# Moving TensorE's operands to the head of SBUF, on multiples of 64 bytes, in a local-attention and FFN kernel

## The chip, the cores and the metric

The kernel runs on one core of one Trainium2 chip. The metric is the device time of one execution in microseconds (us). The kernel before takes 646.3 us, the median of 3 runs (646.12 to 647.43).

## What is computed

One sequence of 2,048 rows with 640 features goes through a layer norm. The normed rows feed two branches: local attention with 32 heads of 20 features, where each row attends to 8 rows at distances 0, 2, ..., 14 back, and a feed-forward network with 1,536 hidden features. The second branch gates the first.

```python
xn = layernorm(x)                                   # 2048 x 640
q, k, v = split(xn @ wqkv)                          # 640 -> 3 x 640, 32 heads of 20
logits[s, w] = q[s] . k[s - 2*w] * 20**-0.5         # w = 0..7, masked where s - 2*w < 0
s = (softmax(logits) @ v) @ wo                      # 640 -> 640
g = silu(silu(xn @ w1) @ w2)                        # 640 -> 1536 -> 640
out = x + s * g
```

Everything is float32 outside the kernel.

## The kernel before

**Tiling.** The rows are taken in 4 groups of 512 (2 halves, 2 parities, since the attention steps by 2). Within a group a row sits on one of 128 partitions and in one of T = 4 column blocks.

**Products in three parts.** To keep float32 accuracy with TensorE's one-pass float32r products, each operand is split into a high half (rounded to float32r) and a low half (the rest), and each product is made of three matmuls: high by high, low by high, high by low. TH and TL hold the two halves of the transposed activations (5 chunks of 128 features, 512 rows each), SH and SL those of the hidden FFN values (two of each, for even and odd chunks f), and the 7 weight slots WR hold a weight chunk's high half in columns 0 to 639 and its low half in columns 640 to 1279. TensorE reads nothing else but the transposes' operands (`ident`, XIN and O).

**The stages of a group g** and their matmuls (stationary operand, moving operand):

- `qkv_phase` (lines 589 to 591, and 541 for the first quarter): TH or TL stationary in blocks of 128 rows, a weight slot moving with 480 columns; 960 matmuls in all.
- `wo_phase` of the group before (lines 623 and 625, through `tm_mm`): TH or TL stationary, a weight slot moving, cut in 384 and 256 columns because a product row of 640 does not fit one PSUM bank. `wo_last` does the same for the last group, and its last block (line 712) runs 15 matmuls of 256 columns after 15 of 384.
- `ffn_phase`: first layer (lines 740 to 742) with 128 columns of a weight slot stationary and TH or TL moving with 512 columns; 720 matmuls. Second layer (lines 623 and 625) with SH or SL stationary and a weight slot moving in 384 and 256 columns. The `wo` and second-layer products together are 816 matmuls of 384 columns and 816 of 256, nearly always in turn.
- Transposes (lines 411, 514, 522): 190 of 128 columns, in float32, with XIN, O or `ident` stationary and `ident` moving.

That is 3,502 matmuls, of which 3,312 are float32r. Each is issued with a weight load of its own (3,502 rows on the PEld engine of the profile).

**Other engines.** VectorE (DVE) does the attention itself (scores at lines 459 and 462, values at 491 and 496), the low halves (416, 530, 356, 748), and the last products with the gate. ScalarE (ACT) writes the high halves (415, 526, 354, 746) and the activations. Weights come from HBM once, are split into halves by ACT and DVE (the first ten by ACT and GpSimd, POOL), stored as halves in HBM (SyncE's queue, SP) and reloaded by POOL's queue (line 346) for later groups.

**The order.** A planner, the class `Weave`, gets every operation with its engine, an estimated duration, what it reads and writes, and a priority; it simulates the five engines and emits every engine's instructions in the resulting order. TensorE's own order is that in which the operations were added. A matmul of n columns is estimated at `n / 2400 + 0.0155` us (`mm`). The planner sees names of tiles, not addresses.

**Addresses.** All SBUF tiles come from one pool, `sb`, with one buffer per tile. Addresses are given out in the order in which the lines of `local_attention_silu_ffn` allocate the tiles; each size is rounded up to 32 bytes. So the order of the lines 188 to 213 is the layout. The first tile, `ident`, starts at byte 16512 of each partition, and `epst`, of 4 bytes, at 17024. In the built program the operands of the float32r matmuls start here:

| tiles | first byte before | modulo 64 | modulo 256 |
|---|---|---|---|
| TH0, TH1, TL0, TL1 | 93984 to 124704 | 32 | 32 |
| SH0, SL0 | 149280, 151328 | 32 | 32 |
| SH1, SL1 | 153632, 155680 | 32 | 32 |
| weight slots 0 to 6 | 188128 to 218848 | 32 | 224 |

The slices that a matmul reads start at a multiple of 512 bytes in TH, TL, SH and SL, and at 0, 1536, 2560 or 4096 bytes (or, as stationary operand, at a multiple of 512) in a slot, so they have the same remainders as the tiles. `ident` is on a multiple of 64; XIN, O and nearly all other tiles are at 32 modulo 64.

Of the kernel before, what the change touches and what calls it, by code (L numbers as in the profile page):

```python
# [8 lines left out]
F32 = mybir.dt.float32  # L9
F32R = mybir.dt.float32r  # L10
# [4 lines left out]
P = 128  # L15
S, D, F, H, DH = 2048, 640, 1536, 32, 20
W = 8
DC, FC = D // P, F // P
NQ = 4
HQ = H // NQ  # L20
CQ = HQ * DH
J = 8
T = 4
TOK = T * P
# [5 lines left out]
RING = 7  # L30
# [134 lines left out]
def local_attention_silu_ffn(ctx: ExitStack, tc: tile.TileContext, x, wqkv, wo, w1, w2, out):  # L165
    nc = tc.nc
    pool = lambda name, bufs, **kw: ctx.enter_context(tc.tile_pool(name=name, bufs=bufs, **kw))
    sb = pool("sb", 1)
# [16 lines left out]
    def tiles(name, n, shape, dtype=F32):  # L185
        return [sb.tile(shape, dtype, name=f"{name}{i}") for i in range(n)]

    ident = sb.tile([P, P], F32, name="ident")
    epst = sb.tile([P, 1], F32, name="epst")
    mask = sb.tile([P, T, W], F32, name="mask")  # L190
    KV = tiles("kv", NQ, [P, 2, HALO + T, CQ])
    Q = tiles("q", NQ, [P, T, CQ])
    O = sb.tile([P, T, D], F32, name="o")
    TH = tiles("th", 2, [P, DC, TOK], F32R)
    TL = tiles("tl", 2, [P, DC, TOK], F32R)
    PR = sb.tile([P, 2, W, CQ], F32, name="pr")
    L = tiles("l", 2, [P, T, W, HQ])
    E = tiles("e", 2, [P, T, W, HQ])
    SH = [sb.tile([P, TOK], F32R, name="sh0")]
    SL = [sb.tile([P, TOK], F32R, name="sl0")]  # L200
    M = tiles("m", 2, [P, T, HQ])
    SH.append(sb.tile([P, TOK], F32R, name="sh1"))
    SL.append(sb.tile([P, TOK], F32R, name="sl1"))
    Z = tiles("z", 2, [P, 2, T, HQ])
    XIN = sb.tile([P, T, D], F32, name="xin")
    ST = tiles("st", 2, [P, 2, 6])
    MV = sb.tile([P, T, 2], F32, name="mv")
    SD = sb.tile([P, 2, T], F32, name="sd")
    G = sb.tile([P, T, D], F32, name="gate")
    XR = tiles("xr", 2, [P, D])  # L210
    SF = tiles("sf", 2, [P, TOK])
    WR = tiles("w", RING, [P, 2 * D], F32R)
    RAW = tiles("raw", 2, [P, D])
    ACC = [psum.tile([P, TOK], F32, name=f"acc{i}") for i in range(6)]
    ROT = [psum.tile([P, TOK], F32, name=f"rot{i}") for i in range(2)]
# [23 lines left out]
    def dve(n, fn, reads, writes, prio, lock=False):  # L239
        add("DVE", dv(n), fn, reads, writes, prio, lock)  # L240

    def act(n, fn, reads, writes, prio, table=None):
        add("ACT", ac(n), fn, reads, writes, prio, table=table)

    def pe(dur, fn, reads, writes):
        add("PE", dur, fn, reads, writes)
        clock[0] += dur
# [52 lines left out]
    def width(u):  # L300
        return 3 * CQ if u[0] == "q" else D
# [31 lines left out]
    def w_load():  # L333
# [5 lines left out]
        n = width(u)  # L339
        r = WR[s]  # L340
        both = r.rearrange("p (s d) -> p s d", s=2)[:, :, :n]
# [26 lines left out]
    def w_next(*want):  # L368
# [4 lines left out]
        s, n = i % RING, width(want)  # L373
        return WR[s][:, :n], WR[s][:, D:D + n], ("wh", s), ("wl", s)

# [9 lines left out]
    def ln_stats(t, after=()):  # L385
        st = ST[t % 2]
        ks = ("st", t % 2)
        for k in range(2):
            dve(320, lambda k=k: nc.vector.bn_stats(out=st[:, k, :], in_=XIN[:, t, k * 320:(k + 1) * 320]),
                [("xin", t), *after], [ks + (k,)], 1)  # L390
        dve(60, lambda: nc.vector.bn_aggr(out=MV[:, t, :], in_=st), [ks + (0,), ks + (1,)], [("mv", t)], 1)

    def ln_rstd(a, b):
        n = range(a, b)
        act(b - a, lambda: nc.scalar.activation(SD[:, 0, a:b], MV[:, a:b, 1], AF.Sqrt, bias=epst, scale=1.0),
            [("mv", t) for t in n], [("sd", t) for t in n], 0, "sqrt")
        dve(10, lambda: nc.vector.reciprocal(out=SD[:, 1, a:b], in_=SD[:, 0, a:b]),
            [("sd", t) for t in n], [("rs", t) for t in n], 1)

    def ln_apply(t):  # L400
        dve(320, lambda: nc.vector.tensor_scalar(  # L401
            out=XIN[:, t, :], in0=XIN[:, t, :], scalar1=MV[:, t, 0:1], scalar2=SD[:, 1, t:t + 1],
            op0=OP.subtract, op1=OP.mult), [("rs", t), ("mv", t)], [("xin", t)], 1, lock=True)

    def split_t(src, skeys, c, i):
# [6 lines left out]
        pe(0.54, turn, skeys, [kp])  # L412
        hi, lo = TH[i][:, c, :], TL[i][:, c, :]
        kh, kl = t_keys(i, [c], kinds=["th"]), t_keys(i, [c], kinds=["tl"])
# [5 lines left out]
    def evac_qkv(g, q, t, ps, kp):  # L420
        kv, qq = KV[q], Q[q]
        act(2 * CQ, lambda: nc.scalar.activation(
# [4 lines left out]
    def halo(g, q):  # L427
        h, par = groups[g]
        kv = KV[q]
        own = kv[:, :, HALO:, :]  # L430
# [22 lines left out]
    def scores(g, q):  # L453
        i = q % 2
        l, e, m, kv, qq = L[i], E[i], M[i], KV[q], Q[q]
        hk = halo_keys(q)
# [19 lines left out]
    def values(g, q):  # L476
        i = q % 2
        e, z, kv = E[i], Z[i], KV[q]
        hk = halo_keys(q)
# [28 lines left out]
    def first_quarter(i):  # L508
# [8 lines left out]
        def turn(t):  # L517
# [6 lines left out]
            for a, b, tp, kp in parts:  # L524
                v = tp[:, :(b - a) * P].rearrange("p (c n) -> p c n", n=P)
                act((b - a) * P, lambda a=a, b=b, v=v: nc.scalar.activation(TH[i][:, a:b, tsl(t)], v, AF.Copy),
                    [kp], t_keys(i, range(a, b), [t], ["th"]), 0)
            for a, b, tp, kp in parts:
                v = tp[:, :(b - a) * P].rearrange("p (c n) -> p c n", n=P)
                dve((b - a) * P, lambda a=a, b=b, v=v: nc.vector.tensor_tensor(  # L530
                    out=TL[i][:, a:b, tsl(t)], in0=v, in1=TH[i][:, a:b, tsl(t)].bitcast(F32), op=OP.subtract),
                    [kp] + t_keys(i, range(a, b), [t], ["th"]), t_keys(i, range(a, b), [t], ["tl"]), 0)

        def products(t, part):
            o, kp = ps[t]
            for k in part:
                for c in range(DC):
                    x, kx = (TL, "tl") if k == 1 else (TH, "th")
                    wh, wl, kh, kl = ws[c]
# [35 lines left out]
    def qkv_phase(g, i, io):  # L575
        for q in range(NQ):
            if g == 0 and q == 0:
                ps = first_quarter(i)
            else:
                ps = [bank() for t in range(T)]  # L580
                for c in range(DC):
                    wh, wl, kh, kl = w_next("q", q, c)
                    for t in range(T):
                        o, kp = ps[t]

                        def unit(c=c, t=t, o=o, wh=wh, wl=wl):
                            o = o[:, :3 * CQ]
                            hi, lo = TH[i][:, c, tsl(t)], TL[i][:, c, tsl(t)]
                            nc.tensor.matmul(o, hi, wh, start=c == 0, stop=False)  # L589
# [6 lines left out]
            if g == 0:  # L596
                add("POOL", 2.0, lambda q=q: nc.gpsimd.memset(KV[q][0:2, :, 0:HALO, :], 0.0), ["first"] if q else [],
                    [("halo", q, 1, 0), ("halo", q, 2, 0), ("halo", q, 3, 0), ("halo", q, 4, 0)], 1 + q)
# [42 lines left out]
    def wo_phase(g, i):  # L641
        banks = tm_banks()
        a, b = banks
        for c in range(DC):
            wh, wl, kh, kl = w_next("wo", c)
            for t in range(T):
                def one(c=c, t=t, wh=wh, wl=wl):
                    tm_mm(banks, t, TH[i][:, c, tsl(t)], wh, c == 0, False)
                    tm_mm(banks, t, TH[i][:, c, tsl(t)], wl, False, False)
                    tm_mm(banks, t, TL[i][:, c, tsl(t)], wh, False, c == DC - 1)  # L650
                pe(3 * TM, one, t_keys(i, [c], [t]) + [kh, kl], [a[t][1], b[t // 2][1]])
# [14 lines left out]
    def wo_last(g, i):  # L666
# [22 lines left out]
        def whole(t, cols):  # L689
            for k in range(3):  # L690
                for c in range(DC):
                    st = (TH, TH, TL)[k][i][:, c, tsl(t)]
                    tm_mm(banks, t, st, ws[c][k == 1], k + c == 0, k == 2 and c == DC - 1, cols)
# [23 lines left out]
    def ffn_phase(g, i, ix, io):  # L717
        nxt = g + 1 if g + 1 < NG else None
        ps = prev = None
        for f in range(FC + 1):  # L720
# [11 lines left out]
            if f < FC:  # L732
# [11 lines left out]
                w_done()  # L744
                sf, sh, sl = SF[s], SH[s], SL[s]
                act(TOK, lambda sh=sh, h=h: nc.scalar.activation(sh, h, AF.Silu), [kp], [("sh", s)], 0, "silu")  # L746
# [35 lines left out]
    add("POOL", 0.7, consts, [], ["consts"], 0)  # L782
    act(1, lambda: nc.scalar.activation(SD[:, 1, 0:1], epst, AF.Sqrt), ["consts"], [("rs", 0)], 0, "sqrt")
    slot = 0
# [38 lines left out]
```

## Time and profile before

| | |
|---|---|
| median of 3 runs | 646.3 us |
| the profiled execution, by its own clock | 645.65 us |
| its span, first to last instruction | 643.9 us |
| PE busy | 637.7 us, 3,502 matmuls |
| PEld busy (weight loads) | 577.3 us, 3,502 loads |
| DVE busy | 537.3 us |
| ACT busy | 206.5 us |
| POOL busy | 125.3 us |
| granted TensorE clock, mean | 0.999 |

How to read it: a matmul's duration in the profile (say 337 ns for 384 columns) reaches from its start to the modelled end of its last result, and overlaps the next matmul's. What a matmul costs in a row of matmuls is the step from its start to the next one's start. The timeline gives starts to 0.01 us from the start of the span; the trace holds them to 1 ns, and where a mean step is given it is taken over these.

### The profile page before, as it was taken

The numbers are of one execution on the slowest core, as the hardware profiler recorded it, in microseconds if no ns is written. First come the engines' busy times: TensorE is split into PE (matmuls) and PEld (weight loads), VectorE is DVE, ScalarE is ACT, GpSimd is POOL, SyncE is SP. The second block draws the span as 40 slices with busy tenths as digits, with TensorE's granted clock in tenths as the row PEclk, the third lists the DMA queues.
The fourth block names the chain that finished last, engine by engine and source line by source line (L and its number), as shares of the span: only waits on it lengthen the run. The fifth ranks groups of instructions, "written<-read, shape, count | busy, mean of one in ns | idle before, by whom it ended". The sixth has DMA issues, their size and how long they took to land.

```text
span 643.9 us, 9033 instructions
## 1 busy us (share of the span) xinstructions
PE 637.7 (99%) x3502; PEld 577.3 (90%) x3502; DVE 537.3 (83%) x532; ACT 206.5 (32%) x401; POOL 125.3 (19%) x171
## 2 busy tenths in 40 slices
PE   8999999999999999999999999999999999999997
PEld 7888899999889989999888999999988899899897
DVE  6699999999999989998939999999106999899714
ACT  5436453443534032324332122223313222233130
POOL 6410000001101331112222124111122213311100
PEclk9999999999999999999999999999999999999999
DMA  9999999677999988556699989865679996886522
GB/s 270 333 308 325 317 402 399 263 226 222 314 318 322 288 285 267 172 186 207 183 262 279 291 218 302 271 189 159 173 207 263 275 307 198 295 267 199 164 82 81
DMA packets 74010, 162.44 MB, mean 252 GB/s; under 512 B 5632, under 2 KB 46816, under 8 KB 73968
## 3 DMA queue, kind: packets, MB, share of 16 engines
q0 software_dynamic: 26672, 82.58, 45.0%
q1 hardware_dynamic: 47296, 79.29, 39.8%
q8 instruction: 27, 0.44, 0.3%
q14 instruction: 15, 0.12, 0.1%
HBM read 109.55 MB, written 34.16 MB: 223 GB/s over the span
## 4 chain that ended last, share of the span: by engine, by line
PE 98%; DMA 1%; DVE 0%; ACT 0%; SPq 0%; issue 0%
PE acc L623 22%; PE acc L625 15%; PE acc L589 10%; PE acc L590 10%; PE acc L591 10%; PE rot L742 9%; PE rot L740 9%; PE rot L741 9%; PE rot L411 2%; PE acc L541 2%; DMA pr<-in_A_wqkv_dram 1%; PE rot L522 0%; PE rot L712 0%; PE acc L514 0%; DVE xin L401 0%; ACT w L354 0%
## 5 line engine op out<-in xcount | busy, mean ns | idle before, releaser
L623 PE MATMUL acc<-w,sh 128*128 128x384 f32 x384 | 115.0, 337 | 0.0
L589 PE MATMUL acc<-w,th 128*128 128x480 f32 x300 | 114.7, 382 | 0.0
L590 PE MATMUL acc<-w,tl 128*128 128x480 f32 x300 | 113.4, 378 | 0.0
L591 PE MATMUL acc<-w,th 128*128 128x480 f32 x300 | 113.4, 378 | 0.0
L625 PE MATMUL acc<-w,sh 128*128 128x256 f32 x384 | 107.6, 280 | 0.0
L459 DVE TENSOR_TENSOR pr<-q,kv 128x2560 f32<-128x2560 f32 x32 | 91.7, 2864 | 11.4 <-DMA kv<-kv 11.0
L740 PE MATMUL rot<-th,w 128*128 128x512 f32 x240 | 95.8, 399 | 0.0
L742 PE MATMUL rot<-th,w 128*128 128x512 f32 x240 | 94.8, 395 | 0.0
L741 PE MATMUL rot<-tl,w 128*128 128x512 f32 x240 | 94.3, 393 | 0.0
L491 DVE TENSOR_TENSOR pr<-e,kv 128x2560 f32<-128x2560 f32 x32 | 90.3, 2821 | 0.7
L462 DVE TENSOR_REDUCE l<-pr 128x128 f32<-128x2560 f32 x32 | 90.0, 2813 | 0.2
L346 POOL DMA_DIRECT2D w<-half_q x52 | 37.3, 717 | 234.2 <-DMA raw<-in_A_wqkv_dram 93.6
L746 ACT ACTIVATE sh<-rot 128x512 fp32r<-128x512 f32 x48 | 28.7, 598 | 162.2 <-PE rot L742 162.1
L496 DVE TENSOR_TENSOR pr<-pr 128x1280 f32<-128x1280 f32 x64 | 79.3, 1240 | 1.1
L346 POOL DMA_DIRECT2D w<-half_w x72 | 38.5, 535 | 181.7 <-PE acc L625 101.3
L625 PEld LDWEIGHTS acc<-w,sh 128*128 128x128 f32 x384 | 72.2, 188 | 1.8
L623 PEld LDWEIGHTS acc<-w,sh 128*128 128x128 f32 x384 | 72.0, 188 | 1.7
L591 PEld LDWEIGHTS acc<-w,th 128*128 128x128 f32 x300 | 56.3, 188 | 8.5
L590 PEld LDWEIGHTS acc<-w,tl 128*128 128x128 f32 x300 | 56.3, 188 | 8.0
L589 PEld LDWEIGHTS acc<-w,th 128*128 128x128 f32 x300 | 56.3, 188 | 8.0
L623 PE MATMUL acc<-w,sl 128*128 128x384 f32 x192 | 58.7, 336 | 0.0
L742 PEld LDWEIGHTS rot<-th,w 128*128 128x128 f32 x240 | 45.1, 188 | 10.3
(84 smaller groups left out, 980.6 us busy)
## 6 DMA issues: line engine op xcount, KB each, us to landing
w<-half_w POOLq DMA_DIRECT2D x72, 640.0 KB, 5.6
w<-half_q POOLq DMA_DIRECT2D x52, 480.0 KB, 4.9
half_w<-w SPq DMA_DIRECT2D x24, 640.0 KB
half_q<-w SPq DMA_DIRECT2D x20, 480.0 KB
w<-half_wo POOLq DMA_DIRECT2D x15, 640.0 KB, 5.0
kv<-kv SPq DMA_DIRECT2D x16, 560.0 KB
kv<-kv SPq DMA_DIRECT2D x16, 420.0 KB
gate<-in_B_w_dram SPq DMA_DIRECT2D x16, 320.0 KB
```

Source lines behind the costliest of these rows:

```text
L459: dve(2560, lambda t=t: nc.vector.tensor_tensor(out=PR, in0=win(qq[:, t:t + 2, :], W, 0), in1=win(kv[:, 0, t:t + 2, :], W, CQ), op=OP.mult ...
L462: dve(2560, lambda t=t: nc.vector.tensor_reduce(out=l[:, t:t + 2].rearrange("p t w h -> p (t w h)"), in_=PR.rearrange("p t w (h d) -> p (t ...
L491: dve(2560, lambda t=t, v=v: nc.vector.tensor_tensor(out=PR.rearrange("p t w (h d) -> p t (w h) d", d=DH), in0=e[:, t:t + 2].rearrange("p ...
L496: dve(2 * n * CQ, lambda n=n: nc.vector.tensor_tensor(out=PR[:, :, 0:n, :], in0=PR[:, :, 0:n, :], in1=PR[:, :, n:2 * n, :], op=OP.add), [] ...
L589: nc.tensor.matmul(o, hi, wh, start=c == 0, stop=False)
L590: nc.tensor.matmul(o, lo, wh, start=False, stop=False)
L591: nc.tensor.matmul(o, hi, wl, start=False, stop=c == DC - 1)
L623: nc.tensor.matmul(a[t][0][:, :CA], st, w[:, :CA], start=first, stop=last)
L625: nc.tensor.matmul(b[t // 2][0][:, h * CB:(h + 1) * CB], st, w[:, CA:], start=first and h == 0, stop=last, skip_group_check=True)
L740: nc.tensor.matmul(h, wh[:, cs], TH[i][:, c, :], start=c == 0, stop=False)
L741: nc.tensor.matmul(h, wh[:, cs], TL[i][:, c, :], start=False, stop=False)
L742: nc.tensor.matmul(h, wl[:, cs], TH[i][:, c, :], start=False, stop=c == DC - 1)
```

## The change

Only the order of the allocations changes. `mv` (32 bytes) and `st0` (64) are put behind `epst`, so that TH starts at 17152; TH, TL and the seven slots follow, then SH1, SL1, `st1`, SH0, SL0, and behind them all the other tiles.

```diff
     ident = sb.tile([P, P], F32, name="ident")
     epst = sb.tile([P, 1], F32, name="epst")
+    MV = sb.tile([P, T, 2], F32, name="mv")
+    ST = [sb.tile([P, 2, 6], F32, name="st0")]
+    TH = tiles("th", 2, [P, DC, TOK], F32R)
+    TL = tiles("tl", 2, [P, DC, TOK], F32R)
+    WR = tiles("w", RING, [P, 2 * D], F32R)
+    SH = [None, sb.tile([P, TOK], F32R, name="sh1")]
+    SL = [None, sb.tile([P, TOK], F32R, name="sl1")]
+    ST.append(sb.tile([P, 2, 6], F32, name="st1"))
+    SH[0] = sb.tile([P, TOK], F32R, name="sh0")
+    SL[0] = sb.tile([P, TOK], F32R, name="sl0")
+    SD = sb.tile([P, 2, T], F32, name="sd")
     mask = sb.tile([P, T, W], F32, name="mask")
+    M = tiles("m", 2, [P, T, HQ])
+    Z = tiles("z", 2, [P, 2, T, HQ])
     KV = tiles("kv", NQ, [P, 2, HALO + T, CQ])
     Q = tiles("q", NQ, [P, T, CQ])
     O = sb.tile([P, T, D], F32, name="o")
-    TH = tiles("th", 2, [P, DC, TOK], F32R)
-    TL = tiles("tl", 2, [P, DC, TOK], F32R)
     PR = sb.tile([P, 2, W, CQ], F32, name="pr")
     L = tiles("l", 2, [P, T, W, HQ])
     E = tiles("e", 2, [P, T, W, HQ])
-    SH = [sb.tile([P, TOK], F32R, name="sh0")]
-    SL = [sb.tile([P, TOK], F32R, name="sl0")]
-    M = tiles("m", 2, [P, T, HQ])
-    SH.append(sb.tile([P, TOK], F32R, name="sh1"))
-    SL.append(sb.tile([P, TOK], F32R, name="sl1"))
-    Z = tiles("z", 2, [P, 2, T, HQ])
     XIN = sb.tile([P, T, D], F32, name="xin")
-    ST = tiles("st", 2, [P, 2, 6])
-    MV = sb.tile([P, T, 2], F32, name="mv")
-    SD = sb.tile([P, 2, T], F32, name="sd")
     G = sb.tile([P, T, D], F32, name="gate")
     XR = tiles("xr", 2, [P, D])
     SF = tiles("sf", 2, [P, TOK])
-    WR = tiles("w", RING, [P, 2 * D], F32R)
     RAW = tiles("raw", 2, [P, D])
```

In the built program after the change TH, TL, the slots, SH1 and SL1 start at 0 modulo 256, and SH0 and SL0 at 64 modulo 256. All the large tiles of the other engines (KV, Q, O, PR, L, E, XIN, `gate`, XR, SF, RAW) start at 224 modulo 256, so again at 32 modulo 64. The instructions of all five engines, their order and their waits are the same ones as before; only addresses differ. PSUM and HBM are laid out as before.

## The prediction

> **What bounds the kernel now.** I read the page first: the busy times, the granted clock, and the chain of work that ended last.
>
> ```profile
> PE 637.7 (99%) x3502; PEld 577.3 (90%) x3502; DVE 537.3 (83%) x532; ACT 206.5 (32%) x401; POOL 125.3 (19%) x171
> PEclk9999999999999999999999999999999999999999
> PE 98%; DMA 1%; DVE 0%; ACT 0%; SPq 0%; issue 0%
> ```
>
> PE is busy without a gap, at the full clock, and is 98% of the chain. Second, the list of waits of PE alone:
>
> ```profile
> PE rot L514 <- POOL ident masks.py:199: 1.4, 1, 1.4
> PE rot L522 <- DVE xin L401: 1.1, 1, 1.1
> ```
>
> Those are all, both in the first 8 us. Afterwards PE waits for no engine and no DMA, so the time is the sum of the steps from one matmul's start to the next one's. Third, the timeline of PE, to see what a step is (columns: start, duration, engine, line, operands). Two stretches of the second FFN layer of group 0, both with SH0 (chunks f = 2 and f = 6), and one of the qkv products:
>
> ```profile
> 85.49 0.34 PE L623 MATMUL acc<-w,sh 128*128 128x384 f32 x1
> 85.67 0.28 PE L625 MATMUL acc<-w,sh 128*128 128x256 f32 x1
> ...
> 86.39 0.34 PE L623 MATMUL acc<-w,sh 128*128 128x384 f32 x1
> ```
>
> ```profile
> 113.59 0.33 PE L623 MATMUL acc<-w,sh 128*128 128x384 f32 x1
> 113.76 0.28 PE L625 MATMUL acc<-w,sh 128*128 128x256 f32 x1
> ...
> 114.45 0.33 PE L623 MATMUL acc<-w,sh 128*128 128x384 f32 x1
> ```
>
> ```profile
> 195.57 0.37 PE L590 MATMUL acc<-w,tl 128*128 128x480 f32 x1
> 195.78 0.38 PE L591 MATMUL acc<-w,th 128*128 128x480 f32 x1
> 195.99 0.38 PE L589 MATMUL acc<-w,th 128*128 128x480 f32 x1
> 196.21 0.38 PE L590 MATMUL acc<-w,tl 128*128 128x480 f32 x1
> 196.43 0.38 PE L591 MATMUL acc<-w,th 128*128 128x480 f32 x1
> 196.65 0.37 PE L589 MATMUL acc<-w,th 128*128 128x480 f32 x1
> ```
>
> Three pairs of 384 and 256 columns take 0.90 us in the first stretch (300 ns a pair) and 0.86 in the second (287), although nothing differs but the weight slot, and the slots are alike modulo 512. Five steps of 480 columns take 1.08 us: 216 each, in a cycle of 211, 215, 214, 222, 218. Fourth, the end, where 256-column matmuls run alone:
>
> ```profile
> 638.26 1.32 PE L712 MATMUL rot<-w,th 128*128 128x256 f32 x10
> 639.42 0.73 PE L712 MATMUL rot<-w,tl 128*128 128x256 f32 x5
> ```
>
> One lasts 276 ns, so the five make (730 - 276) / 4 = 113.5 ns a step (113.3 by the starts in ns). Over the whole trace the mean steps are 231.0 ns for 512 columns, 216.0 for 480 and 293.2 for a pair (of 801 pairs 448 are near 287, 307 near 300).
>
> **What a step is made of.** The shortest frequent steps are 211 ns for 480 columns and 171 for 384: 40 ns for 96 columns, 0.417 ns a column. At that rate the columns alone need 213.3 ns (512), 200.0 (480), 266.7 (a pair) and 106.7 (256). What stands above it is 17.7 ns for each of 720 matmuls, 16.0 for 960, 26.5 for 816 pairs: 12.7 + 15.4 + 21.6 = **49.7 us** that are not columns. This fixed part is all that the change can touch on PE.
>
> It has a grain. The repeating steps, 113.3, 286.7, 300.0, 233.3 (the slower of two rhythms of 512 columns) and 1080 for five, are all multiples of 3.33 ns, the time of 8 columns, which is 32 bytes: just what all these operands start off a 64-byte mark. And the tail's 113.3 is 106.7 + 6.6, or 16 columns, 64 bytes, to within the clock of the trace.
>
> **The change, part by part.**
>
> 1. *Instructions, waits, queues.* None is added, removed or moved; no wait changes its engine. Cost nothing, by comparison of the two instruction lists.
>
> 2. *The moving operand on a 64-byte mark* (slots for 480, 384 and 256 columns, TH and TL for 512). No row shows a float32r operand on such a mark, so the price is bounded. One end is nothing: a stream that starts 32 bytes off costs no more than an aligned one. The far end is the whole fixed part, 49.7 us. A value between: if PE takes its stream in 64-byte pieces, a run of 16m columns covers m pieces when aligned and m + 1 when off, and the extra piece costs 16 columns, 16 x 0.417 = 6.7 ns. The nearest row, the tail at 106.7 + 6.6, shows just that, and no product's steps repeat at less than 6 ns above their columns. I take it: 3,312 x 6.7 ns = **22.1 us**.
>
> 3. *The stationary operand on a 64-byte mark.* Here rows exist, in float32: at half clock, weight loads of `ident` (aligned) and of XIN (32 off) both last 230 ns and the transposes step by 213.3 both times; at full clock those of XIN and O step by 108.4. So I take nothing. Bounds: no loss is excluded, since moving and stationary streams now start alike (0 and 0 modulo 256, before 224 and 32); a gain could be at most what part 2 leaves of the 49.7 us.
>
> 4. *Tiles of DVE, ACT and POOL.* Their remainder modulo 64 stays 32. I take nothing. Were DVE 1% slower or faster (5.4 us), its idle 106.6 us (643.9 - 537.3) and the slack of part 6 would hide it.
>
> 5. *DMAs.* A slot's destination goes from 224 to 0 modulo 256, the attention tiles from 32 to 224. A reload lands 5.6 us after issue (median) and PE never waits for one: nothing. Only the opening is uncovered: the first 10 us include loads of `pr` that make up the chain's 1% DMA; were these 5% longer or shorter, it would be 0.3 us, an estimate.
>
> 6. *What is late next.* DVE's order is fixed, and in the stretch from 32 to 322 us it is busy 274.7 of 290. If PE gets 3.4% faster (22.1 of 645.65), that stretch shrinks to 280, and DVE still fits. From 338 to 450 it is busy 108.4 of 112, which shrinks to 108.2: full, but each SL is written 2 to 8 us before PE reads it, and DVE idles behind it (3.4 us busy between 450 and 483). At the end, the last O is written 6.7 us before its transposes at 614 us; DVE works on that chain from 483, PE's 131 us shrink by 4.5, leaving 2.2. I put 1 us of new waits in the sum; with the fixed part wholly gone it would be 3 or 4.
>
> **Sum**, against the profiled execution's own 645.65 us (span 643.9): 645.65 - 22.1 + 1.0 = 624.6. The median of the runs is 0.65 higher, so I forecast **625.2 us**. If only the 8 columns of the offset are paid instead of 16, it is 11 us less gain: 636.
>
> **The rivals.**
>
> *No change (646).* The grain of 32 bytes may be the chip's own piece, or only its clock; then 32 modulo 64 was aligned already. For it: the aligned and unaligned weight loads of part 3 are alike, and the two pair rhythms of 287 and 300 ns occur with the same addresses modulo 512, so much of the fixed part is rhythm, not address. The Trainium skill speaks for this case: "SBUF — State Buffer", in the section on Door 1, gives SBUF lines of 16 bytes, on which all operands of the kernel before already start; by that the sum would be 645.65 - 0. No run here shows such a line.
>
> *A bigger gain (605).* Both streams pay a piece: 2 x 6.7 x 3,312 = 44.4 us, less 3.5 us of DVE waits: 605.4. For it: the loads of float32r operands last 188 ns, those of float32 140, so that path is not the one of part 3. Against it: part 3. The Trainium skill, "TensorE: Matmul & The Clock Gate", section on the back-to-back issue gap, has warm bf16 matmuls step by N/2.4 + 2.5 ns, 215.8 for 512 columns where this trace has 231.0; by that rule all but 3,312 x 2.5 = 8.3 us of the 49.7 would go, 604.3 before waits.
>
> *Slower (653).* The fixed part depends on how a matmul's stream falls against the next one's weight load, which starts some 3 ns after it (PEld and PE starts). The trace shows two rhythms for the same work: 287 or 300 ns a pair, 229 or 233.3 for 512 columns. With all operands on one remainder the pairs may lock to the slow one: 801 x (300 - 293.2) = 5.4 us and 720 x (233.3 - 231.0) = 1.7 us, 645.65 + 7.1 + 0.65 = 653.4; were the 480-column steps all at the 222 of their cycle, 960 x 6 = 5.8 us more, 659. It decides as soon as the slow share of pairs, now 307 of 801, rises and the piece of part 2 is not real. Against it: the rhythm now follows the history and not an address (SH0's pairs are slow at f = 2 and fast at f = 6).
>
> **How the numbers follow.** The forecast's case, between 612 and 640, gets 0.38; the bigger gain 0.12; no change 0.14; slower 0.36, of which a quarter beyond 655. The range 605 to 655 leaves out about 0.07 below and 0.09 above. Faster by over 0.2% (about what a measurement of this kernel can tell from no change): 0.38 + 0.12 = 0.50.
>
> **What would show it.** The 480-column steps should fall from 216 to about 209 ns, those of 512 from 231 to 224, the pair from 293 to 280, the tail from 113.3 to 107 or to the 108.4 of the transposes, where weight loads may bind. If the steps move by 13 ns, both streams pay; if they stay and the time too, 64 is not the number; if the pairs all read 300, the rhythm decided. PE's list of waits should stay near 2.5 us; rows of DVE there would mean that part 6 was too mild.

## The result and the profile after

The changed kernel takes **644.0 us** (median of 6 runs, 643.8 to 644.53), the one before beside it 646.57 (6 runs, 646.12 to 647.43): a ratio of **0.9959, 95% interval 0.9946 to 0.9972**. The forecast had the direction and eight times the size: 21 us were expected, 2.6 came. A later comparison made it smaller still (last experiment).

The page of the changed kernel: busy times, granted clock, chain.

```profile
PE 635.4 (99%) x3502; PEld 576.0 (90%) x3502; DVE 536.6 (83%) x532; ACT 206.1 (32%) x401; POOL 126.5 (20%) x171
PEclk8999999999999999999999999999999999999999
PE 98%; DMA 1%; DVE 0%; ACT 0%; SPq 0%; issue 0%
```

The list of waits of PE, whole:

```profile
PE rot L523 <- DVE xin L402: 2.3, 1, 2.3
PE rot L515 <- POOL ident masks.py:199: 1.4, 1, 1.4
```

PE is still the only bound, it waits for nothing after the opening, and its busy time is 2.3 us less. So the difference is in the steps. The timeline of PE in the changed kernel (start, duration, engine, line, operands) at the places shown for the one before: second FFN layer with SH0 at f = 2 and f = 6, and qkv products (the seventh step's end is the last line).

```profile
85.59 0.34 PE L624 MATMUL acc<-w,sh 128*128 128x384 f32 x1
...
86.46 0.33 PE L624 MATMUL acc<-w,sh 128*128 128x384 f32 x1
...
113.69 0.34 PE L624 MATMUL acc<-w,sh 128*128 128x384 f32 x1
...
114.55 0.33 PE L624 MATMUL acc<-w,sh 128*128 128x384 f32 x1
```

```profile
150.20 0.38 PE L592 MATMUL acc<-w,th 128*128 128x480 f32 x1
...
151.72 0.37 PE L590 MATMUL acc<-w,th 128*128 128x480 f32 x1
```

Three pairs take 0.87 and 0.86 us, so both stretches run at 287 to 290 ns a pair. Over the whole trace the mean pair hardly moved: 293.2 ns before, 292.8 now. Seven steps of 480 columns take 1.52 us, 217 each: not the 209 that the forecast wanted but slightly more than before. The steps that fell are those of 512 columns, here in one steady stretch of each kernel (not at the same place of the order), the changed one first and an execution of the one before (run `b2` below) second:

```profile
112.26 0.39 PE L742 MATMUL rot<-tl,w 128*128 128x512 f32 x1
...
113.17 0.39 PE L743 MATMUL rot<-th,w 128*128 128x512 f32 x1
```

```profile
75.65 0.40 PE L741 MATMUL rot<-tl,w 128*128 128x512 f32 x1
...
76.58 0.40 PE L742 MATMUL rot<-th,w 128*128 128x512 f32 x1
```

Four steps: 0.91 us against 0.93, 227 against 233 ns. Over the whole traces the mean steps went from 231.0 to 228 ns (512 columns) and from 216.0 to 216.8 (480). The tail went the wrong way too:

```profile
638.27 0.76 PE L713 MATMUL rot<-w,tl 128*128 128x256 f32 x5
```

Five matmuls of 256 columns take 0.76 us where they took 0.73: 120 ns a step by the starts, before 113.3.

**What the steps follow.** Call the *distance* of a matmul the first byte of its moving operand less that of its stationary one, modulo 256. The change did not only bring the operands to multiples of 64, it also changed the distances:

| | before | after |
|---|---|---|
| 480 columns, `wo` pairs (slot over TH, TL) | 192 | 0 |
| 512 columns (TH, TL over slot) | 64 | 0 |
| pairs over SH1, SL1 | 192 | 0 |
| pairs over SH0, SL0 | 192 | 192 |

Three theories went into the experiments. **Mark**: the remainder modulo 64 of an operand sets the step (the forecast). **Distance**: the distance does. **History**: the same operations fall into different rhythms by how a stretch is entered, whatever the addresses.

The time of each part of PE's order, in us, from the starts in the traces (matmuls 0 to 109; the rest of qkv; FFN without its last ten matmuls; `wo` of groups 0 to 2; those ten and `wo_last` up to its last block; that block and the end), for the kernels of this document:

| kernel | opening | qkv | FFN | `wo` 0-2 | last `wo` | rest | span |
|---|---|---|---|---|---|---|---|
| before, first trace | 25.16 | 201.00 | 341.56 | 52.90 | 15.00 | 8.27 | 643.88 |
| before, `b1` | 25.21 | 201.00 | 341.46 | 54.46 | 15.00 | 8.29 | 645.42 |
| before, `b2` | 25.36 | 201.00 | 341.54 | 54.45 | 15.00 | 8.29 | 645.64 |
| before, `b3` | 24.94 | 201.00 | 341.40 | 54.48 | 15.00 | 8.29 | 645.11 |
| before + 32 bytes, `e2` | 24.72 | 201.02 | 341.10 | 52.15 | 15.00 | 8.27 | 642.26 |
| after | 25.67 | 201.66 | 339.15 | 53.34 | 14.66 | 8.29 | 642.76 |
| after, `a2` | 24.64 | 201.66 | 339.17 | 54.05 | 14.66 | 8.29 | 642.48 |
| after + 32 bytes, `e1` | 24.99 | 201.61 | 339.42 | 54.30 | 14.66 | 8.29 | 643.28 |
| `x1`, all SH at 192 | 25.20 | 201.66 | 338.42 | 53.32 | 14.70 | 8.30 | 641.60 |
| `x2`, all SH at 0 | 25.28 | 201.62 | 340.22 | 53.32 | 14.66 | 8.27 | 643.38 |
| `x3`, slots 128 from TH | 25.39 | 203.51 | 344.65 | 52.13 | 14.37 | 8.30 | 648.36 |
| `x4`, qkv weights at 12 | 25.01 | 199.35 | 338.46 | 53.30 | 14.70 | 8.30 | 639.11 |
| `x5`, qkv weights at 36 | 26.01 | 207.56 | 338.40 | 53.25 | 14.70 | 8.32 | 648.23 |

The opening varies by 1 us between executions of one kernel (25.67 and 24.64 of after), so it is left out of the readings. Nor is all of the `wo` column steps of PE. The second matmul of each of the three stages is held until ACT has emptied the PSUM bank that it writes, as the waits of the weight loads (PEld) show, here in the kernel before:

```profile
PEld acc L625 <- ACT q L425: 0.8, 3, 0.3
```

That is about 0.25 us for each stage. In `b3`, `a2` and `e1` the hold of the first stage is longer, and PE itself waits 0.7, 0.6 and 0.9 us there. The first `wo` stages of `a2` and `e1` take 18.50 and 18.75 us by this, where all the other stages of the two, and of the changed kernel's first trace, take 17.76 to 17.79.

### The profile page after: what moved, and what is told of

Its sections match the earlier page's. It is cut to its first block, busy times and chain, and to the rows that moved or that the text cites. A ratio compares the mean times of both kernels' runs of the same rounds, so it can differ in the third digit from the quotient of the medians.

```text
span 642.8 us, 9033 instructions
## 1 busy us (share of the span) xinstructions
PE 635.4 (99%) x3502; PEld 576.0 (90%) x3502; DVE 536.6 (83%) x532; ACT 206.1 (32%) x401; POOL 126.5 (20%) x171
## 4 chain that ended last, share of the span: by engine, by line
PE 98%; DMA 1%; DVE 0%; ACT 0%; SPq 0%; issue 0%
PE acc L624 22%; PE acc L626 15%; PE acc L590 10%; PE acc L592 10%; PE acc L591 10%; PE rot L742 9%; PE rot L743 9%; PE rot L741 9%; PE rot L412 2%; PE acc L542 2%; DMA pr<-in_A_wqkv_dram 1%; PE rot L523 0%; PE rot L713 0%; PE acc L515 0%; DVE xin L402 0%; ACT w L355 0%
## 5 line engine op out<-in xcount | busy, mean ns | idle before, releaser
L460 DVE TENSOR_TENSOR pr<-q,kv 128x2560 f32<-128x2560 f32 x32 | 90.2, 2820 | 11.4 <-DMA kv<-kv 10.9
L741 PE MATMUL rot<-th,w 128*128 128x512 f32 x240 | 94.9, 395 | 0.0
L743 PE MATMUL rot<-th,w 128*128 128x512 f32 x240 | 93.7, 391 | 0.0
L492 DVE TENSOR_TENSOR pr<-e,kv 128x2560 f32<-128x2560 f32 x32 | 90.3, 2821 | 0.7
L497 DVE TENSOR_TENSOR pr<-pr 128x1280 f32<-128x1280 f32 x64 | 76.5, 1195 | 1.1
L417 DVE TENSOR_TENSOR tl<-rot,th 128x512 fp32r<-128x512 f32 x35 | 23.9, 682 | 36.4 <-ACT th L416 36.3
```

The source lines that it names most:

```text
L460: dve(2560, lambda t=t: nc.vector.tensor_tensor(out=PR, in0=win(qq[:, t:t + 2, :], W, 0), in1=win(kv[:, 0, t:t + 2, :], W, CQ), op=OP.mult ...
L492: dve(2560, lambda t=t, v=v: nc.vector.tensor_tensor(out=PR.rearrange("p t w (h d) -> p t (w h) d", d=DH), in0=e[:, t:t + 2].rearrange("p ...
L497: dve(2 * n * CQ, lambda n=n: nc.vector.tensor_tensor(out=PR[:, :, 0:n, :], in0=PR[:, :, 0:n, :], in1=PR[:, :, n:2 * n, :], op=OP.add), [] ...
L741: nc.tensor.matmul(h, wh[:, cs], TH[i][:, c, :], start=c == 0, stop=False)
L743: nc.tensor.matmul(h, wl[:, cs], TH[i][:, c, :], start=False, stop=c == DC - 1)
```

## The experiments

**The mark alone, both ways (`e1`, `e2`).** Every float32r operand 32 bytes further on, off the mark in the changed kernel and onto it in the one before, all distances kept.

```diff
# e1, in the changed kernel
+    pad0 = sb.tile([P, 8], F32, name="pad0")
     TH = tiles("th", 2, [P, DC, TOK], F32R)
...
+    pad1 = sb.tile([P, 8], F32, name="pad1")
     SD = sb.tile([P, 2, T], F32, name="sd")
# e2, in the kernel before
+    pad0 = sb.tile([P, 8], F32, name="pad0")
     mask = sb.tile([P, T, W], F32, name="mask")
```

> The kernel after with 32 bytes put ahead of TH and 32 ahead of SD: all float32r operands start 32 bytes off a 64-byte mark again, but keep their distances from each other; the other large tiles stay at 32 modulo 64. Theory M (the 64-byte mark counts): the steps go back to those of before, 231 ns for 512 columns and 216.0 for 480, time about 646.5. Theory D (the distance between the moving and the stationary start, modulo 64, 128 or 256, counts): the steps stay as after, near 228 for 512 and 216.8 for 480, time about 644. Theory H (no address counts, only the history of the opening): any mixture.

> The kernel before with 32 bytes put ahead of mask: all tiles move by 32 bytes, so the float32r operands stand on 64-byte marks, with the distances of before (weight slots 192 bytes behind TH, modulo 256). Theory M: steps as after, 228 ns for 512 columns and 216.8 for 480, about 644. Theory D: steps as before, 231 and 216.0, about 646.5. Theory H: any mixture.

Measured: `e1` 644.58 us (5 runs), ratio to the kernel before 0.9957 (0.9943 to 0.9971), and `e2` 644.14 us (4 runs, 643.94 to 644.44), ratio 0.9958 (0.9943 to 0.9973). The steps stay with the distances: 480 columns 216.7 ns in `e1` (216.8 after), 216.02 in `e2` (216.0 before); 512 columns 229.0 (228.2 after) and 230.7 (231.0). So the mark moves no step, and the theory behind the forecast falls. What `e2` did gain is mostly in one column of the table: `wo` takes 52.15 us where `b2` takes 54.45. The timeline of PE in the `wo` stage of group 1, `e2` first, then `b2`, then the changed kernel:

```profile
362.79 0.33 PE L624 MATMUL acc<-w,th 128*128 128x384 f32 x1
...
363.65 0.33 PE L624 MATMUL acc<-w,th 128*128 128x384 f32 x1
```

```profile
365.25 0.34 PE L623 MATMUL acc<-w,th 128*128 128x384 f32 x1
...
366.15 0.34 PE L623 MATMUL acc<-w,th 128*128 128x384 f32 x1
```

```profile
363.62 0.34 PE L624 MATMUL acc<-w,tl 128*128 128x384 f32 x1
...
364.50 0.34 PE L624 MATMUL acc<-w,tl 128*128 128x384 f32 x1
```

Three pairs take 0.86, 0.90 and 0.88 us. `e2` and `b2` both have the distance 192 and still differ, 287 and 300 ns a pair; the changed kernel, at 0, has 293. Here history counts.

**TensorE alone (`m1`, `m2`, `m3`, `m4`).** Programs that leave out all of the reference's work (x is copied to the output) and in which only TensorE works, in rows of equal matmuls, with three transposes between rows: start offsets of both operands (`m1`), sizes and types (`m2`), the distance in steps of 4 bytes and beyond 256 and the entry of pairs (`m3`), all 64 distances (`m4`).

```diff
# m4, the rows of one distance m
+    for m in range(0, 256, 4):
+        row((512,), m, 0, 26)
+        row((480,), m, 0, 26)
+        row((384, 256), m, 0, 14, 512)
+        row((384, 256), m, 0, 14, 400)
```

> Nothing of the reference's work is done: x is copied to the output, and TensorE runs rows of 10 to 16 float32r matmuls of 512, 480, 384 and 256 in turn, and 384 columns, with the moving operand and the stationary operand each starting at 0, 32, ..., 224 bytes modulo 256 (64 combinations for each size), three transposes apart. Theory M: the step depends on each start modulo 64 alone; combinations with both on a mark are the shortest. Theory D: the step depends on the difference of the two starts and is the same along each diagonal. Theory H: the steps are alike in all 64 to about 1 ns, or differ without order. If the other engines are what makes the fixed part, all steps here come near n x 0.417 + 2 or 3 ns (215 for 512).

> Nothing of the reference's work is done: x is copied to the output, and TensorE runs rows of 24 float32r matmuls of 128 to 512 columns in steps of 32, of 512, 480, 384 and 256 columns with 32, 64 and 96 stationary columns, and of bf16 operands, each with both starts at 0 and at 32 bytes. If the fixed part of a step is a piece of the moving stream, it is the same 7 ns for any number of stationary columns and appears only at 32. If it comes from the weight load that runs beside the matmul, it shrinks with the stationary columns: from about 17 ns at 128 to about 13, 9 and 4 at 96, 64 and 32. If it belongs to float32r's four bytes, bf16 shows 2 to 3 ns.

> Nothing of the reference's work is done. TensorE runs rows of 22 float32r matmuls of 512 and of 480 columns with the stationary operand at 0 and the moving one at 0, 4, ..., 64 bytes and at 128 to 1024, and rows of 14 pairs of 384 and 256 columns at distances 192, 0 and 32, each row after 3 matmuls of another size (256 to 512 columns in steps of 16) that shift its entry. Theory D with a period of 256 bytes: distances 256, 512, 768 and 1024 read like 0, and 320 like 64 (512 columns: 227, 227, 227, 227, 229). If the operands are read in pieces of 16 or 32 bytes, all starts within a piece read alike. At distance 192 some entries settle at 287 ns a pair and others at 300, at distance 0 all near 293.5 and at 32 all near 291.3; if 287 and 300 do not come from the entry, all rows at 192 are alike.

> A program of TensorE work alone (x is copied to the output, none of the reference's work is done): for the 64 distances d = 0, 4, ..., 252 bytes from the stationary operand's start to the moving one's, a row of 26 steps of 512 columns, one of 26 steps of 480, and 14 pairs of 384 + 256 columns after a lead of 512 and after one of 400. Distance theory: the steps repeat what the earlier program of this kind gave at the same distances (512 columns: 226.7 at 0, 240.0 at 20, 226.6 at 28 and 60, 233.4 at 128; 480 columns: 216.7 at 0, 213.4 at 12 and 44, 223.0 at 36), all on the grain of 3.33 ns, and there are distances at which 720 x the 512 step at -d, 960 x the 480 step and 240 x the pair at d come to less than at 0. Mark theory: every d that leaves the moving operand off a multiple of 64 costs the same, above the four that leave it on one (0, 64, 128, 192). History theory: the same distance gives other steps in another order of rows, by over 3 ns in the mean.

Measured in `m1`, over 8 x 8 start offsets: at most distances the step depends on the difference of the two starts and not on either. At distance 0 the 480 columns step by 216.6 to 216.7 ns for all eight starts, and rows of 512 settle at 226.7 for seven of them, after some ten uneven steps of 224 to 237 (the eighth was the program's first row and ran at 427). At a few distances equal rows settle at different steps: 480 columns at 224 take 213.3, 216.6 or 220.0. The steady steps in ns, the multiples of 32 from `m1`, the others from `m3` and `m4`:

| distance | 0 | 12 | 20 | 28 | 36 | 64 | 128 | 192 |
|---|---|---|---|---|---|---|---|---|
| 512 columns | 226.7 | 228.9 | 236 to 240 | 226.7 | 234.7 | 229.0 | 233.1 | 233.4 |
| 480 columns | 216.6 | 213.4 | 219.9 | 213.4 | 223.1 | 218.3 | 217.6 or 220 | 216.0 |
| pair 384 + 256 | 293.3 | 290.0 | 303.3 | 290.0 | 300.0 | 293.3 | 286.6 or 300 | 286.6 or 300 |

Adding 256 to the distance changes nothing (480 columns: 216.6 at every multiple; 512: 226.7 at 0, 256, 512, 768 and 1024). In `m3` and `m4` the stationary operand always starts at 0, so for offsets under 32 bytes it is carried over from `m1`, and not tried, that the difference counts and not the moving start. The timeline of PE in `m4`: at distance 20 a row of 26 matmuls of 512 columns, one of 26 of 480, one of 14 pairs; then the same at 28.

```profile
135.77 6.38 PE L80 MATMUL acc<-mv,st 128*128 128x512 f32 x26
...
142.24 5.97 PE L80 MATMUL acc<-mv,st 128*128 128x480 f32 x26
...
149.09 4.40 PE L80 MATMUL acc<-mv,st 128*128 128x384 f32 x28
...
181.45 6.16 PE L80 MATMUL acc<-mv,st 128*128 128x512 f32 x26
...
187.69 5.80 PE L80 MATMUL acc<-mv,st 128*128 128x480 f32 x26
...
194.35 4.23 PE L80 MATMUL acc<-mv,st 128*128 128x384 f32 x28
```

Eight bytes are worth 0.22 us in 25 steps of 512 columns, 9 ns each, and neither 20 nor 28 is a multiple of 64, nor of 16. The kernel's steps agree with the map: 480 columns 216.0 before (216.0 at 192) and 216.8 after (216.6 at 0), 512 columns 231.0 and 228.2 (229.0 and 226.7; the kernel's rows have 15 matmuls and are in part uneven entry). The tail agrees too: `m2` has 256 columns at distance 0 at 120.0 ns a step, on the mark and off it.

At 128 and 192 the pairs have two rhythms. In `m3` a pair row at 192 had three matmuls of one of 17 sizes ahead of it: after 256, 272, 320, 336, 352, 400 or 480 columns it ran at 286.6 to 286.8 ns to its end, after 288, 304, 368, 384, 416, 432, 448, 464, 496 or 512 at 300.0. At distance 0 all were at 293.0 to 294.0. So history is real, but only at certain distances; 128 and 192 are not the only ones (in `m4`, at 104, a pair takes 300.2 ns after a lead of 512 columns and 326.6 after one of 400).

Timeline of PE in `m2`: 480 and 512 columns with both operands on the mark, then both 32 bytes off it, then 480 columns in bf16.

```profile
69.62 5.45 PE L81 MATMUL acc<-mv,st 128*128 128x480 f32 x24
75.15 5.74 PE L81 MATMUL acc<-mv,st 128*128 128x512 f32 x24
...
122.28 5.44 PE L81 MATMUL acc<-mv,st 128*128 128x480 f32 x24
127.80 5.71 PE L81 MATMUL acc<-mv,st 128*128 128x512 f32 x24
...
253.21 5.02 PE L81 MATMUL acc<-mvb,stb 128*128 128x480 bf16 x24
```

On the mark or off it, these rows of float32r last the same to 0.03 us. Of the sizes from 224 to 512 only 448 differs by more than 1.4 ns a step, 202.7 on the mark and 206.7 off it; that was not run again. In bf16 the steady step is the columns at 0.417 ns and 2.5 ns more (202.5 for 480, 215.8 for 512, 55.8 for 128); in float32r 13 to 17 ns more between 256 and 512 columns except 11.7 at 288 and 16 to 20 at 448, and never under 111.6. With 32 stationary columns in place of 128 the weight load lasts 108 ns in place of 188, and 512 columns step by 231.7, 480 by 213.3, 384 by 173.4 (with 128: 226.7 to 228.1, 216.7, 173.3): the fixed part is not the length of the load.

**The distance of the FFN pairs (`x1`, `x2`).** In the changed kernel `st1`, 64 bytes, lies between SL1 and SH0, which gives the odd chunks distance 0 and the even ones 192. `x1` puts it ahead of SH1 (192 for all), `x2` behind SL0 (0 for all).

```diff
# x1; in x2 the line goes behind the allocation of SL[0]
+    ST.append(sb.tile([P, 2, 6], F32, name="st1"))
     SH = [None, sb.tile([P, TOK], F32R, name="sh1")]
     SL = [None, sb.tile([P, TOK], F32R, name="sl1")]
-    ST.append(sb.tile([P, 2, 6], F32, name="st1"))
     SH[0] = sb.tile([P, TOK], F32R, name="sh0")
```

> The kernel after with st1 ahead of SH1 instead of ahead of SH0, so that all four FFN halves start 64 bytes past the slots modulo 256 (distance from stationary to moving 192), as SH0 and SL0 do already. In the kernel after, pairs of 384 and 256 columns with SH0 and SL0 take 288.1 ns on average and those with SH1 and SL1 (distance 0) 293.5. Theory D (the distance modulo 256 sets the step): the pairs of SH1 and SL1 fall to 287 to 288, 288 x 5.6 ns = 1.6 us, time about 642.4. Theory M (both starts on a 64-byte mark is all that counts) and theory H (history alone): no change, 644.

> The kernel after with st1 behind SL0, so that all four FFN halves start at the slots' remainder modulo 256 (distance 0). Theory D: the pairs of SH0 and SL0 rise from 288.1 to about 293.5 ns, 288 x 5.4 ns = 1.6 us, time about 645.6. Theories M and H: 644.

Measured: `x1` 643.4 us, ratio 0.9943 (0.993 to 0.9955), `x2` 644.68, ratio 0.9965 (0.9952 to 0.9977), on the same chip beside the same runs of the kernel before (647.31 us); 1.28 us apart where 3.2 were expected. The pairs did as the map says: those over SH1 and SL1 go from 294.1 to 290.0 ns in `x1`, those over SH0 and SL0 from 289.3 to 293.7 in `x2` (means of all pairs). Part of it comes back in the 512 steps, which start each row from the pairs' end: 229.0 in `x1`, 227.9 in `x2`. FFN is 338.42 against 340.22 us.

**A distance that is bad on marks (`x3`).** 128 bytes ahead of the slots: every operand stays on a multiple of 64, and TH and slots lie 128 apart.

```diff
+    pad0 = sb.tile([P, 32], F32, name="pad0")
     WR = tiles("w", RING, [P, 2 * D], F32R)
```

> The kernel after with 128 bytes put ahead of the weight slots: every float32r operand is still on a 64-byte mark, but TH and the slots are 128 bytes apart modulo 256; SH, SL and the slots keep their distances. Theory D, by the table of offsets without the other engines (512 columns 227.8 ns at distance 0 and 233.1 at 128; 480 columns 216.4 and 218.8): 720 x 5.2 + 960 x 2.2 = 5.9 us more, and the pairs of the wo products at 287 or 300 instead of 293.5, up to 1.6 us either way: 648.3 to 651.5, slower than before. Theory M: 644. Theory H: 643 to 647.

Measured: 649.99 us, ratio 1.0044 (1.003 to 1.0057), **slower than the kernel before, with all operands on the mark**. 480 columns step by 218.9, 512 by 232.3, as the map has them for 128. The `wo` pairs, at 128, run in the short rhythm (287.0), while those over SH0, still at 192, entered the long one, here at f = 2:

```profile
86.23 0.34 PE L625 MATMUL acc<-w,sh 128*128 128x384 f32 x1
...
87.13 0.34 PE L625 MATMUL acc<-w,sh 128*128 128x384 f32 x1
```

Three pairs, 0.90 us; in the changed kernel 0.87 at the same chunk with the same distance.

**One distance alone, both signs (`x4`, `x5`).** The qkv weights fill 480 of the 640 columns of each half of a slot. On top of `x1` they are put 12 or 36 bytes further on in it; no tile moves.

```diff
+AT = 3      # x5: 9
...
+    def base(u):
+        return AT if u[0] == "q" else 0
...
-        both = r.rearrange("p (s d) -> p s d", s=2)[:, :, :n]
+        both = r.rearrange("p (s d) -> p s d", s=2)[:, :, a:a + n]
...
-        return WR[s][:, :n], WR[s][:, D:D + n], ("wh", s), ("wl", s)
+        return WR[s][:, a:a + n], WR[s][:, D + a:D + a + n], ("wh", s), ("wl", s)
```

> The kernel with ST1 ahead of SH1 (643.4 us), and the qkv weights, which fill 480 of a slot's 640 columns, 12 bytes further on in their slots: no byte more is taken, no other operand moves. Distance theory: the 960 steps of 480 columns go from a distance of 0 (216.8 ns in that kernel) to one of 12, where the program of TensorE work alone gave 213.4: 960 x 3.4 = 3.3 us less, 640.1 us, a ratio of 0.989 to 0.990; the steps of 512 and the pairs stay (228.3 to 228.9; 287 to 293). Mark theory: the qkv weights now start off every multiple of 64, and a moving operand off the mark costs 6.7 ns a step as in the prediction: 960 x 6.7 = 6.4 us more, 649.8. History theory: the 480 steps stay within 1 ns of 216.8 whatever the 12 bytes.

> The same edit with 36 bytes in place of 12. Distance theory: the steps of 480 columns go to the 223.3 ns that the program of TensorE work alone gave at 36, 960 x 6.5 = 6.2 us more than the kernel it is built on: 649.6 us, a ratio of 1.003 to 1.005 to the kernel before, and 9.5 us above the kernel with 12 bytes. Mark theory: 12 and 36 are both off the mark, so the two kernels take the same time. History theory: the steps stay within 1 ns of 216.8.

Measured: `x4` **640.88 us** (5 runs, 640.22 to 641.04), ratio 0.9936 (0.9923 to 0.9948), `x5` 648.92, ratio 1.0064 (1.0051 to 1.0078), beside runs of the kernel before with a median of 644.95. PE's timeline in the second quarter of group 1, `x4`, then `x5`:

```profile
150.18 0.38 PE L594 MATMUL acc<-w,th 128*128 128x480 f32 x1
...
151.67 0.38 PE L595 MATMUL acc<-w,tl 128*128 128x480 f32 x1
```

```profile
153.28 0.39 PE L595 MATMUL acc<-w,tl 128*128 128x480 f32 x1
...
154.84 0.39 PE L596 MATMUL acc<-w,th 128*128 128x480 f32 x1
```

Seven steps in 1.49 and in 1.56 us. Over the traces the 480 columns step by 214.1 ns (213.4 expected) and 223.3 (223.3), while 512 and the FFN pairs stay within 0.2 ns of `x1`. Mark and history theory both wanted the two kernels alike; they are 8.0 us apart (9.1 by the spans, 8.2 of it in qkv). Distance decides.

`x4` is the best kernel here: its runs end below all of the changed kernel's (643.58 to 645.45 in two comparisons). Ratios to the kernel before cannot be set beside each other across comparisons, since its own median lay between 644.83 and 647.31. PE's busy time is lowest too:

```profile
PE 632.9 (99%) x3502; PEld 575.6 (90%) x3502; DVE 535.9 (84%) x532; ACT 206.0 (32%) x401; POOL 128.7 (20%) x171
```

**What the kernel before is measured against (`b1`, `b2`, `b3`, `a2`).** The kernel before three times more for its trace, the changed one once more; no edit.

> The kernel before once more, unchanged, for a second trace. Its profiled execution took 645.65 us, the median of its other runs is 647.0. If the difference is the rhythm of the pairs (287 or 300 ns at distance 192, by what came before), this trace has another share of slow pairs, in whole stages (a wo stage 17.4 or 18.2 us, the last FFN with wo 99.7 or 100.1), and the same steps of 512 and 480 columns. If it is the opening, the stages after 25 us agree to 0.1 us and the opening differs.

> The kernel before, unchanged, for its trace: wo stages of the groups 0 to 2 (120 matmuls each) and the time. If the rhythm of the wo stages makes the spread of its runs, the time is 644.8 + 0.78 x the number of the three stages that take 18.15 instead of 17.38 us, to within 0.5 us. If the spread comes from elsewhere (the opening, the qkv stages), the times differ with the same stages.

> Once more the same, on the same chip: 644.8 + 0.78 x the number of slow wo stages, to within 0.5 us; or, if the spread comes from elsewhere, not.

> The changed kernel, unchanged, beside more runs of the one before. If its gain of 2.6 us is the difference of distances alone, the ratio is 0.996 on every chip. If part of it is that the kernel before entered its wo stages in the slow rhythm, the changed kernel stays at 643.5 to 644.6 us, and the difference is 2.3 to 2.9 us where the runs of the kernel before lie at 646 to 647.5, and 0.8 or less where they lie at 644 to 645.

Measured: 647.19, 647.4 and 646.89 us for the kernel before. In `b1` and `b2` all three `wo` stages are in the long rhythm (18.15 us each; the first trace, 645.65 us, had one long and two short ones of 17.38). Qkv and last `wo` agree to 0.01 us and FFN to 0.16, so the 1.5 us in `wo` carry the difference. `b3` has only two long stages. Its first takes 18.18 us because PE waits there, once, for ACT:

```profile
PE acc L625 <- ACT q L425: 0.7, 1, 0.7
```

Behind that wait its pairs run at 287 ns, the short rhythm. So `b3` fits the formula expected for it (647.14 with three slow stages) by chance: with the two that it has, the formula gives 646.36. This one stage also suggests that the moment at which ACT lets PE in is part of the entry. `a2`: the changed kernel 644.16 us (11 runs) beside 15 runs of the one before with a median of 644.83 (643.78 to 646.52): ratio **0.9988 (0.9979 to 0.9997)**. There the gain is 0.67 us, as expected for a kernel before that enters its `wo` stages in the short rhythm. Those 15 runs have no trace, so that they did is argued, not shown; and why `b2` and `b3`, on the same chip, came out above all of them stays open.

The table says what is distance: after against `b2` without the opening is -3.2 us (qkv +0.66, FFN -2.39, `wo` -1.11, last `wo` -0.34). With `wo` of the kernel before at its short rhythm in all three stages (3 x 17.38 = 52.1) the term of `wo` turns to +1.2, and the sum to -0.9. So of these 3.2 us, 0.9 are better distances, and 2.3 come from a rhythm that the kernel before falls into at distance 192 and that distance 0 does not have. That the 2.6 us of the first comparison divide likewise is argued: of the kernel before it has one trace, that of the 645.65 us with one long stage.

## Why the prediction was wrong, point by point

- **What bounds the kernel** was right: PE 98% of the chain, before and after. "Afterwards PE waits for no engine" holds for the list of PE's own waits that it shows, and not quite for the steps: the hold by ACT makes the first pair of each `wo` stage 456 ns long, about 0.5 us in all. That 49.7 us are not columns was right as a size: `m2` finds 13 to 17 ns per float32r matmul with no other engine at work.
- **The step that failed is part 2**: "if PE takes its stream in 64-byte pieces, a run of 16m columns covers m pieces when aligned and m + 1 when off, and the extra piece costs 16 columns, 16 x 0.417 = 6.7 ns". No such piece shows: in `m2` 256, 384, 480 and 512 columns step alike to 1.4 ns on the mark and off it, `e1` and `e2` keep their steps when all operands move by 32. The term of 22.1 us measures, as a sum over qkv, FFN and `wo`, between 0.9 and 3.2 us, and has another cause. The numbers that carried it, 3.33 ns as a grain and 113.3 = 106.7 + 6.6 in the tail, were true; that the grain was *bytes of an offset* was read into them. The tail itself, the row taken as nearest, rose to 120 ns on the mark.
- **Part 3** put the stationary operand at nothing, because weight loads of `ident` and XIN last the same. ("At half clock" is read from the steps of the transposes, 213.3 against 108.4 ns; the granted clock of the profile is 1.00 over the first 10 us.) The duration of a load says nothing of the step: in `x1` only SH and SL move, as stationary operands, and their pairs change by 4 ns. It is the remark beside it that was on the track: "moving and stationary streams now start alike (0 and 0 modulo 256, before 224 and 32)"; the forecast gave it no price.
- **Parts 1, 4 and 5** (nothing for instructions, other engines, DMAs): PE's list of waits is as short as before, 3.7 us against 2.5, all in the opening. The score products of DVE took 2864 ns on average in the first trace and 2821 after the change, but two other traces of the kernel before have 2820 and 2821, so nothing shows that the layout did it. **Part 6** was not put to the test, since PE got too little faster to crowd DVE; in `x4`, 3.7 us of span faster than after, PE's waits stay two, 2.5 us together. The waits that did come up behind the opening, in `b3`, `a2` and `e1`, are for ACT and not for DVE, and the kernel before has one too.
- **The rivals.** *No change (646)* came nearest, and its reason held in part: "much of the fixed part is rhythm, not address". Its other half, that 32 modulo 64 was aligned already, is what `e1` and `e2` show. The 16-byte lines that it cited from the Trainium skill, "SBUF — State Buffer", do not set the step either: at the multiples of 16, 480 columns step by 216.6 (0), 216.7 (16), 217.9 or 220.0 (32) and 213.3 (48). *The bigger gain* fell with the mark. The rule beside it, N/2.4 + 2.5 ns of the Trainium skill, "TensorE: Matmul & The Clock Gate", in the section on the back-to-back issue gap, holds here for bf16 (`m2`: 202.5 and 215.8 against 202.5 and 215.8 by the rule) and for no row in float32r (at best 213.3 and 226.6). *Slower (653)* named the right kind of mechanism, rhythms that lock, at a price that `x3` has paid at another distance: 649.99 us with the pairs over SH0 at 300 and 512 columns at 232.3. At distance 0 the pairs lock to one rhythm as that rival said, but to 293 and not to the 300.
- **What would show it** did its work: 209, 224, 280 and 107 ns were named, and 216.8, 228, 292.8 and 120 stood in the trace. The line "if they stay and the time too, 64 is not the number" is the one that came true.

## What to carry to other kernels

In a kernel whose PE is never idle, compare addresses of the two operands of a matmul with each other, not with a power of two: here one offset of 12 bytes inside a weight slot gave 2.3 us in qkv, more than the 0.9 us that the distances of a whole new layout gave, and 36 bytes cost 8 us against it. Before pricing an alignment, take two stretches of the trace that differ in it alone, or run rows of matmuls with only the offset changed; one such program would have replaced the forecast's 22 us. And where a stage has two rhythms, look at several traces of the kernel before, since a comparison may measure the rhythm that it happened to enter.

## What the runs showed of the hardware that was not expected

- A float32r matmul's step depends on the distance of its two operands' starts, modulo 256 bytes and with a grain of 4: 226.7 to 240.0 ns for 512 columns, 213.3 to 223.4 for 480, 288 to 313.4 for a pair of 384 + 256 with one rhythm. What in TensorE or SBUF makes this is not settled; two operand streams that meet in the same place would fit, and is only argued.
- At distances 128 and 192 the pair has two rhythms, 286.6 and 300.0 ns, chosen by the matmul ahead of it and kept for the rest of the row.
- Float32r weight loads last 188 ns (128 columns) against 98 in bf16, and with fewer than 256 moving columns a float32r matmul does not step faster than 111.6 ns.
- `e2` enters its `wo` stages in the short rhythm at the distances of the kernel before: the first pair takes 465 to 469 ns in `e2`, against 455 to 457 where PE does not wait in the kernel before. Perhaps that is because O moved against `ident` as well; it was not tried by itself. How little decides is seen in the first trace, where the first pair of the long stage takes 456 ns and those of the two short ones 455.
